# Linear attention, mixture of experts and gated FFN on one core: squares on ScalarE for the weights' scales, unread products in TensorE's pauses, another planned order

## The chip, the cores and the metric

The kernel runs on one core of one Trainium2 chip. The metric is device microseconds (us) of one execution. TensorE (PE) multiplies; VectorE (DVE), ScalarE (ACT) and GpSimd (POOL) do the element work, SyncE (SP) issues the transfers.

## The reference

```python
q_s = exp(q - max_d q); q_s /= sum_d q_s + 1e-9        # q, k, v: (4, 8, 576, 64)
k_s = exp(k - max_s k); k_s /= sum_s k_s + 1e-9        # over the 576 rows
kv  = einsum('bhsd,bhse->bhde', k_s, v)
x   = einsum('bhsd,bhde->bhse', q_s, kv)               # as (2304, 512)
...
P = exp(x @ w_gate - max); 8 rounds of P /= rows' sums, P /= columns' sums, P *= N / E
out = sum_e P[:, e:e+1] * (relu(x @ w1[e]) @ w2[e])    # 8 experts, 512 -> 1024 -> 512
...
h = out @ w_in; g = h * clip(h + 3, 0, 6) / 6; return g @ w_out    # 512 -> 2048 -> 512
```

## The kernel before, in words

**Arithmetic.** A product of fp32 matrices is three fp16 products of high and low halves, and each 2x2 block product takes seven block products instead of four (the forms QA11 to QS3 of a weight, QB11 to QT3 of its partner). So each operand is scaled by a power of two (`pow2`), split (`split`, `sp`) and added into forms. A scale needs the largest absolute value of the whole operand: VectorE reduces along the rows, `across_max` turns the column round with one PE product and reduces it again.

**Tiling.** The 2304 tokens are 6 groups of 384, taken in three pairs, `PAIRS = [(0, 1), (3, 4), (2, 5)]`. The experts are 16 steps (512 columns of one expert's hidden size each), the FFN 4 more; a step takes the pairs one after the other. The weights of step s come by `w1_steps` and `w2_steps`: a load of 1 MB into `raw`, the scale (`w_scale`, L611), splits and sums into `w1buf[s % 2]` or `w2buf[s % 2]`.

**Head.** `attention(0)` works on batches 0 and 1, `attention(1)` on 2 and 3. For keys: `kmax`, `ktr`, `mT`, `kback` (column maxima by way of PE), `ksub`, `kexp`, then `kv` (PE) and `kvout`, `kvmax`, `kvkeep` (its scale). For queries of a group: `qmax`, `qsub`, `qexp`, `qsum`, then per 128 columns `qn` (the norm), `qtr` (PE transposes into a bank, copied out) and `forms` (products with kv, whose forms are operands of step 0). The second pair's queries and the second two batches run beside step 0 (`beside`, `second_pair`).

**Between experts and FFN.** `x2_steps(p)` takes the scale of pair p's result in `acc` (two reduces of 128x1536 on VectorE), scales, turns it round on PE, splits it and adds the FFN's forms.

**The order** is not that of the code. `Planner` (L42) records every instruction (so nearly all show one line, L376 before, L449 after), and `lay` puts them on each engine's queue by modelled costs (`cost`), hops between engines (`hop`) and latest times (`late`, from the time at which the code reaches a PE instruction, backwards). Steps marked as fill go into gaps. The queues are fixed once this is done: an engine does its queue in order, waiting on semaphores.

```python
# L236, order: latest times, then two layings
late = o["at"] + (0.0 if o["eng"] == "tensor" else 10 * self.SLACK if o["fill"] else self.SLACK)
for b in o["post"]:
    late = min(late, b["late"] - o["dur"] - self.hop(o, b))
# L373, issue
for o in self.order():
    for f, a, k in o["calls"]:
        f(*a, **k)
```

Of the kernel before, what the change touches and what calls it, by code (L numbers as in the profile page):

```python
# [36 lines left out]
TOP1 = 12  # L37
TOP2 = 12
H_DOWN = 2.0 ** -21
# [3 lines left out]
class Planner:  # L43
# [10 lines left out]
    GIVE = 100.0  # L54

# [7 lines left out]
    def __init__(self, nc):  # L63
        self.nc = nc
        self.ops = []
        self.clock = 0.0
        self.sb, self.bank = {}, {}
        self.open = None
        self.filling = False
        for e in self.ENGINES:  # L70
            setattr(self, e, Planner.Lane(self, e))
# [56 lines left out]
    def cost(self, eng, name, out, ins):  # L128
# [4 lines left out]
        if eng == "tensor":  # L133
            four = 4 if ins[0].dtype == F32 else 1
            return 2.0 + n * 0.4167 * four
# [22 lines left out]
    def add(self, eng, name, a, k):  # L158
# [4 lines left out]
        ins = [x for x in rest if isinstance(x, bass.AP)]  # L163
        dur = self.cost(eng, name, out, ins)
# [10 lines left out]
        if op is None:  # L175
            op = dict(
                n=len(self.ops), eng=eng, calls=[call], dur=dur, at=self.clock, pre={}, post=[], key=None,
                lock=False, dma=0, name=name, fill=self.filling, out=out.tensor.name,
            )
            self.ops.append(op)  # L180
        if eng == "tensor":
            op["key"] = key
            self.open = op
            self.clock += dur
# [10 lines left out]
        for x, w in [(i, False) for i in ins] + [(out, True)]:  # L195
# [3 lines left out]
    def touch(self, op, x, w):  # L199
        t = x.tensor.name  # L200
        if x.space == bass.MemoryType.PSUM:
            if op is not self.open:
# [24 lines left out]
    def hop(self, a, b):  # L227
# [4 lines left out]
        if a["eng"] == "sync":  # L232
            return 2500.0 + a["dma"] / 150.0
        return self.HOP + (self.MARGIN if b["eng"] == "tensor" else 0.0)

    def order(self):  # L236
# [6 lines left out]
        for o in reversed(ops):  # L243
            late = o["at"] + (0.0 if o["eng"] == "tensor" else 10 * self.SLACK if o["fill"] else self.SLACK)
            for b in o["post"]:
                late = min(late, b["late"] - o["dur"] - self.hop(o, b))
            o["late"] = late
        first = self.lay([o for o in ops if not o["fill"]], None)
# [4 lines left out]
    def lay(self, ops, first):  # L253
# [8 lines left out]
        lag = shift = 0.0  # L262
# [66 lines left out]
        while len(result) < len(ops):  # L329
# [4 lines left out]
            s, o = best[e]  # L334
            if first and o["fill"]:
# [9 lines left out]
            if e == "sync":  # L345
                free[e] = s + 60.0
                end = s
# [25 lines left out]
    def issue(self):  # L373
        for o in self.order():
# [5 lines left out]
def tile_attention_moe_ffn(  # L380
# [170 lines left out]

    def across_max(c, name, st, exact=False):
# [17 lines left out]
    def pow2(m, dst, top):  # L570

        mc = col("mc")
        nc.vector.tensor_scalar(out=mc, in0=m, scalar1=2.0 ** -60, scalar2=2.0 ** 60, op0=ALU.max, op1=ALU.min)
        eb = col("eb", 1, I32)
        nc.vector.tensor_scalar(
            out=eb, in0=mc.bitcast(I32), scalar1=0x7F800000, scalar2=None, op0=ALU.bitwise_and
        )
# [33 lines left out]
    def w_scale(name, st, out_, top, flat=raw):  # L611
        def am(i):
            def f():
                if i == 0:
                    st["am"] = col(f"am_{name}", 2)
                n = NKC * FS // 2
# [6 lines left out]
        def red():  # L623
            st["m"] = col(f"wm_{name}")
            nc.vector.reduce_max(st["m"], st["am"], axis=AX)

        def fin():
            st["s"] = ring("ws", [P, 2], F32, 8)
            pow2(st["mm"], st["s"], top)

        a, gap, b = across_max(lambda: st["m"], name, st)
        return [am(0), am(1), lambda: (red(), a()), gap, b, fin]
# [5 lines left out]
    def w1_steps(s, first=False):  # L638
# [16 lines left out]
        if first:  # L655
            scale = w_scale(f"a{s}_", st, s, TOP1)
# [9 lines left out]
        steps = [load] + fill(s) + w_scale(f"a{s}_", st, s, TOP1)  # L666
# [10 lines left out]
    def w2_steps(s, flat=raw):  # L677
# [10 lines left out]
        steps = [load] + fill(s) + w_scale(f"b{s}_", st, s, TOP2, flat)  # L688
# [99 lines left out]
    def attention(pr):  # L788
# [47 lines left out]
        def vcopy(c, room):  # L836
            hs = slice(2 * c, 2 * c + 2)
            nc.gpsimd.tensor_copy(
# [117 lines left out]
        def qsub(g, eng=nc.vector):  # L956
# [14 lines left out]
        def qn(c, g):  # L971
# [3 lines left out]
            nc.gpsimd.tensor_tensor(  # L975
# [493 lines left out]
    def down_tile(s, p, grp, t, hs):  # L1469
# [21 lines left out]
        leave(s, j)  # L1491
        tick()


# [317 lines left out]
    def x2_steps(p):  # L1812
# [3 lines left out]
        def am(i):  # L1816
            def f():
                if i == 0:
                    st["am"] = col("x2m", 2)
                nc.vector.tensor_reduce(  # L1820
                    out=st["am"][:, i : i + 1],
# [273 lines left out]
```

## Time and profile before

| | us |
|---|---|
| median of 3 runs (1833.99 to 1836.21) | 1836.21 |
| the profiled execution's own time | 1834.17 |
| its span | 1832.4 |
| PE busy, DVE busy | 1778.7, 1446.7 |
| ACT busy, POOL busy | 1041.5, 616.1 |

The span is what the profiler's rows cover; 1.8 us lie around it in the execution's own time. PE is busy for 97% of it, yet busy says that a product was under way, not at which clock: the granted clock (PEclk, 1.00 is 2.4 GHz, 0.50 is 1.2 GHz) is read beside it. The head before the first expert product, the first step and the passage from experts to FFN differ from the rest, so the stretches have to be read apart.

### The profile page before, as it was taken

To read this page: it belongs to the slowest core of one execution; us is meant where nothing else is said; L and a number is where in the kernel's file an instruction comes from. 1 tells how busy PE (TensorE), PEld (TensorE's weight loads), DVE (VectorE), ACT (ScalarE), POOL (GpSimd) and SP (SyncE) were. 2 spreads that over 40 slices of the span, in tenths; PEclk is the share of its full clock that TensorE was granted. 3 is DMA by queue.
4 is the path that set the end of the run, shared out by engine and by line. 5 is a ranking of instruction groups with operands and counts; after the bars stand their busy time and mean duration, and the time that the engine had idled before them with its cause. 6 is when DMAs were issued, how large, how long until landed. Compare 5 with 4: busy or idle time off the path is not lost.

```text
span 1832.4 us, 32369 instructions
## 1 busy us (share of the span) xinstructions
PE 1778.7 (97%) x12858; PEld 1193.4 (65%) x12858; DVE 1446.7 (79%) x2558; ACT 1041.5 (57%) x2231; POOL 616.1 (34%) x581
## 2 busy tenths in 40 slices
PE   4889999999999999999999999999999989999999
PEld 3445555677777777777777777777775545577775
DVE  6975598987888879787888888786986796888674
ACT  2665555555555656555555555655655665665553
POOL 3322425523333242424343332324242434232121
PEclk8899999999999999999999999999999999999999
DMA  8410213131231312131422323131413102302022
GB/s 257 141 66 1 84 59 97 42 110 64 95 102 58 101 58 84 58 120 40 127 69 88 92 68 101 41 101 58 124 36 112 61 24 84 107 1 84 1 89 75
DMA packets 68664, 145.89 MB, mean 80 GB/s; under 512 B 14624, under 2 KB 18720, under 8 KB 68000
## 3 DMA queue, kind: packets, MB, share of 16 engines
q1 hardware_dynamic: 68512, 143.82, 24.5%
q8 instruction: 100, 1.64, 0.4%
q14 instruction: 52, 0.43, 0.1%
HBM read 119.69 MB, written 24.12 MB: 78 GB/s over the span
## 4 chain that ended last, share of the span: by engine, by line
PE 91%; DVE 7%; ACT 1%; issue 1%; DMA 1%; SPq 0%; POOL 0%; DVEq 0%; ACTq 0%; POOLq 0%
PE b L376 91%; DVE xbuf L376 2%; DVE scr L376 1%; DVE ring_qm L376 1%; DVE acc L376 1%; DVE ring_c L376 1%; DVE w2buf L376 1%; DVE ring_r L376 0%; ACT scr L376 0%; DMA acc<-in_v_dram 0%; DVE w1buf L376 0%; SPq L376 0%; DMA acc<-in_q_dram 0%; DVE prob L376 0%; DVE ring_h L376 0%
## 5 line engine op out<-in xcount | busy, mean ns | idle before, releaser
L376 PE MATMUL b<-xbuf,w1buf 128*128 128x384 f16 x5040 | 911.5, 326 | 7.0 <-DVE ring_r L376 6.9
L376 POOL TENSOR_TENSOR ring_h<-ring_r,ring_h 128x384 f16<-128x384 f32 x360 | 352.6, 981 | 997.5 <-ACT ring_h L376 929.7
L376 PE MATMUL b<-w2buf,ring_h 128*128 128x256 f16 (+1 forms) x3756 | 682.5, 316 | 0.9 <-ACT b L376 0.9
L376 PEld LDWEIGHTS <-w1buf 128*128 128x128 f16 x5040 | 491.6, 98 | 286.8 <-issue 10.2
L376 PEld LDWEIGHTS <-ring_h 128*128 128x128 f16 x4320 | 422.3, 98 | 197.1 <-issue 4.6
L376 ACT COPY b<-b 128x256 f32<-128x256 f32 (+1 forms) x658 | 240.2, 375 | 337.4 <-PE b L376 186.0
L376 DVE SCALAR_TENSOR_TENSOR acc<-b,ring_cf,acc 128x512 f32<-128x512 f32 x369 | 274.9, 749 | 131.6 <-PE b L376 118.8
L376 ACT ACTIVATE ring_r<-b 128x384 f32<-128x384 f32 x432 | 211.8, 491 | 194.4 <-PE b L376 191.3
L376 PEld LDWEIGHTS <-xbuf 128*128 128x128 f16 x2436 | 226.2, 98 | 80.9 <-issue 2.0
L376 DVE SCALAR_TENSOR_TENSOR ring_r<-b,ring_r 128x384 f32<-128x384 f32 x282 | 156.0, 553 | 94.4 <-PE b L376 52.6
L376 ACT ACTIVATE ring_h<-ring_r 128x384 f16<-128x384 f32 x330 | 171.2, 522 | 37.7 <-DVE ring_r L376 33.1
L376 DVE TENSOR_TENSOR xbuf<-ring_h 128x768 f16<-128x768 f16 x188 | 122.5, 652 | 1.2 <-POOL ring_h L376 0.8
L376 PE MATMUL b<-xbuf 64*64 64x65 f32 (+1 forms) x1140 | 101.4, 263 | 3.1 <-POOL xbuf L376 1.8
L376 POOL TENSOR_TENSOR scr<-scr 128x512 f32<-128x512 f32 x64 | 85.1, 1329 | 37.7 <-ACT scr L376 33.3
L376 DVE TENSOR_REDUCE ring_c<-raw 128x1 f32<-128x1024 f32 x78 | 92.1, 1208 | 0.0
L376 ACT ACTIVATE ring_r<-ring_r 128x384 f32<-128x384 f32 x114 | 59.7, 523 | 51.7 <-DVE ring_r L376 51.5
L376 PE MATMUL b<-kvs,xbuf 128*128 128x256 f16 x564 | 84.6, 273 | 0.4 <-ACT b L376 0.4
L376 PE MATMUL b<-scr,xbuf 128*128 128x256 f16 x564 | 84.6, 273 | 0.0
L376 PE MATMUL b<-w2buf,xbuf 128*128 128x256 f16 x564 | 84.6, 273 | 0.0
L376 DVE SCALAR_TENSOR_TENSOR w1buf<-raw,ring_ws,w1buf 128x512 f16<-128x512 f32 x100 | 82.8, 860 | 1.0 <-ACT w1buf L376 0.9
L376 DVE SCALAR_TENSOR_TENSOR acc<-b,ring_co,acc 128x512 f32<-128x512 f32 x78 | 57.9, 748 | 30.8 <-PE b L376 28.5
L376 ACT CAST ring_h<-ring_r 128x384 f16<-128x384 f32 x150 | 74.9, 509 | 11.7 <-DVE ring_r L376 10.3
(148 smaller groups left out, 1575.1 us busy)
## 6 DMA issues: line engine op xcount, KB each, us to landing
xbuf<-xkeep SPq DMA_DIRECT2D x119, 384.0 KB, 3.6
raw<-in_moe_w_dram SPq DMA_DIRECT2D x31, 1024.0 KB, 5.5
xkeep<-xbuf SPq DMA_DIRECT2D x4, 2688.0 KB, 8.1
scr<-in_moe_w_in_dram SPq DMA_DIRECT2D x16, 512.0 KB, 3.7
scr<-in_moe_w_out_dram SPq DMA_DIRECT2D x16, 512.0 KB, 3.4
out_dram<-acc SPq DMA_DIRECT2D x18, 256.0 KB, 2.0
win<-scr SPq DMA_DIRECT2D x16, 256.0 KB, 2.6
wout<-scr SPq DMA_DIRECT2D x16, 256.0 KB, 3.3
```

The costliest lines, as they stand in the source:

```text
L376: f(*a, **k)
```

## The change

1. **Weights' scales.** `w_scale` no longer takes absolute maxima on VectorE (two reduces of 128x1024 per set of weights). ScalarE squares the four 128x512 pieces and sums each row's squares on the way (`accum_out`); the squares themselves go to a buffer of forms that is not yet in use. The four columns are added, turned round as before, and `pow2` halves the exponent. 40 sets of weights: 160 ScalarE instructions for 80 VectorE reduces.
2. **Unread products.** `issue(warm)` looks, in the first 130 us of the plan, for pauses of PE over 0.4 us and puts in products of 256 columns (`ones`, `plus`) into a bank that the next reader does not read: 156 pairs of a weight load and a product (71 ahead of the first `kv`, 42 between the last query transposes and the first `forms`, the others in smaller lots).
3. **Planner.** Transfers are modelled as one queue of 350 B/ns; fp32 passes of PE cost more in the model; of two instructions of DVE and POOL that lock each other out the more urgent goes first; a table moves attention's steps to earlier or later (`EARLIER`, `LATER`).
4. **Placement.** Two of the first four copies of v go to ACT, `qsub` of the first pair from DVE to POOL, `qn` (all but 6 of 24) from POOL to DVE.
5. **FFN's input.** The six reduces of 128x1536 become 18 of 128x512, one after the last addition to each 128 tokens (`largest`); latest times of the first PE steps after it are loosened (`X2_LATE`).

```diff
+EARLIER = {"0kexp": -19500.0, ...
+LATER = {"a1scale": 20000.0}
+X2_LATE = (3000.0, 20000.0, 20000.0)
...
             if e == "sync":
                 free[e] = s + 60.0
+                pipe = max(pipe, s + 2000.0) + o["dma"] / 350.0
+                o["land"] = pipe + 2000.0 - s
...
+                if warm and o["start"] < self.WARM and pause > 400:
...
+                    if b:
+                        best = min(b, key=lambda t: seen[t][1] if t in seen else 0.0)
+                        warm(best, int((pause - 150) * self.FILLED[o["start"] > self.COLD] / 109))
...
-    def w_scale(name, st, out_, top, flat=raw):
-        def am(i):
...
-                nc.vector.tensor_reduce(
-                    out=st["am"][:, i : i + 1], in_=flat[:, i * n : (i + 1) * n], axis=AX, op=ALU.max,
-                    apply_absolute_value=True,
...
+    def w_scale(name, st, rest, flat=raw):
+        junk = view(rest, 0, [P, FS], F16)
+
+        def squares(c):
             def f():
+                if c == 0:
+                    st["sq"] = col(f"sq_{name}", NKC)
+                nc.scalar.activation(
+                    junk, flat[:, c * FS : (c + 1) * FS], AF.Square, accum_out=st["sq"][:, c : c + 1]
                 )
             return f
...
-            nc.vector.reduce_max(st["m"], st["am"], axis=AX)
+            nc.vector.tensor_reduce(out=st["m"], in_=st["sq"], axis=AX, op=ALU.add)
...
-            nc.gpsimd.tensor_copy(
+            (nc.scalar.copy if c in (0, 3) else nc.gpsimd.tensor_copy)(
...
-        def qsub(g, eng=nc.vector):
+        def qsub(g):
+            eng = nc.gpsimd if g in PAIRS[0] else nc.vector
...
-            nc.gpsimd.tensor_tensor(
+            (nc.gpsimd if pr == 0 and c % 2 else nc.vector).tensor_tensor(
                 out=t["qn"].rearrange("p (r h d) -> p h r d", h=2, d=D), in0=qof(g)[:, 2 * c : 2 * c + 2],
...
+        if s == NE - 1:
+            largest(p, j)
...
+        nc.vector.tensor_reduce(
+            out=m[:, len(n) - 1 : len(n)], in_=acc[:, j, :], axis=AX, op=ALU.max, apply_absolute_value=True
+        )
...
-                run(x2_steps(pp))
+                run(loosely(x2_steps(pp), X2_LATE[pp]))
...
+            real.tensor.matmul(banks[t][:, : 2 * P], plus, some, start=True, stop=True, skip_group_check=True)
```

**ScalarE, the head.** `xbuf` holds the keys, of 128x1152 per exponential; `acc` of 128x8x192 are a group's queries, `acc` of 128x18x64 two heads' pieces of v, and `ring_h<-b` the copies of the turned queries. Before:

```order
L376 ACTIVATE xbuf<-xbuf 128x1152 x3
L376 ACTIVATE acc<-acc 128x8x192 x2
L376 ACTIVATE xbuf<-xbuf 128x1152
L376 COPY ring_h<-b_67 128x384 x2
L376 COPY ring_h<-b_68 128x384
```

And now:

```order
L449 ACTIVATE xbuf<-xbuf 128x1152
L449 ACTIVATE w1buf_79,ring_c_107<-raw 128x512 x4
L449 ACTIVATE acc<-acc 128x8x192
L449 COPY xbuf<-acc 128x18x64
L449 ACTIVATE xbuf<-xbuf 128x1152
L449 ACTIVATE acc<-acc 128x8x192
L449 COPY xbuf<-acc 128x18x64
L449 COPY ring_h<-b_68 128x384
L449 COPY ring_h<-b_67 128x384
L449 ACTIVATE xbuf<-xbuf 128x1152
```

The four squares of the first weights and two copies of v now stand between the first and the second of the keys' exponentials, and four copies of queries ahead of the last one.

**VectorE, kv of the second two batches**, beside step 0 (`kvs` is kv's normed result, `w2buf_82` the second weights of step 1, `ring_qm` the queries' maxima and sums). Before:

```order
L376 SCALAR_TENSOR_TENSOR ring_h<-ring_r,ring_h 128x384
L376 TENSOR_SCALAR ring_ws<-ring_c1i 128x1
L376 TENSOR_TENSOR ring_wsc<-ring_ws 128x1
L376 SCALAR_TENSOR_TENSOR w2buf_82<-raw,ring_ws,w2buf_82 128x512 x4
L376 TENSOR_SCALAR ring_c_108<-b_68 128x4
L376 TENSOR_SCALAR ring_c_108<-b_67 128x4
L376 RECIPROCAL ring_c_108<-ring_c_108 128x8
L376 TENSOR_TENSOR kvs_89<-b_68,ring_c_108 128x4x64
```

And now:

```order
L449 TENSOR_TENSOR acc<-acc,ring_qm 128x8x192 x2
L449 SCALAR_TENSOR_TENSOR ring_h<-ring_r,ring_h 128x384
L449 TENSOR_REDUCE ring_qm<-acc 128x8x3 x2
L449 TENSOR_SCALAR ring_c_109<-b_68 128x4
L449 TENSOR_SCALAR ring_c_109<-b_67 128x4
L449 RECIPROCAL ring_c_109<-ring_c_109 128x8
L449 TENSOR_TENSOR kvs_89<-b_68,ring_c_109 128x4x64
```

The four splits of `w2buf_82` and the scale that they need came ahead of the norm of kv and now come some twenty rows behind it, one at a time.

**VectorE, the last pair's passage to the FFN** (`acc<-b` are the last additions of the experts, `sx` is the scale). Before:

```order
L376 SCALAR_TENSOR_TENSOR acc<-b_66,ring_cf,acc 128x512
L376 TENSOR_REDUCE ring_c_103<-acc 128x1
L376 TENSOR_REDUCE ring_c_107<-ring_c_103 128x1
L376 TENSOR_REDUCE ring_c_103<-raw 128x1
L376 TENSOR_REDUCE ring_c_107<-b_67 128x1
```

And now:

```order
L449 SCALAR_TENSOR_TENSOR acc<-b_65,ring_cf,acc 128x512
L449 TENSOR_REDUCE ring_x2m<-acc 128x1
L449 SCALAR_TENSOR_TENSOR acc<-b_66,ring_cf,acc 128x512
L449 TENSOR_REDUCE ring_x2m<-acc 128x1
L449 TENSOR_REDUCE ring_c_108<-ring_x2m 128x1
L449 TENSOR_TENSOR xbuf<-scr,xbuf 128x384 x2
L449 TENSOR_REDUCE ring_c_108<-b_67 128x1
```

The long reduce behind the last addition became a short one, and the reduce of weights in `raw` is gone from between.

## Rows read from the trace of the kernel before

**Rows 1.** Stretches: start and length, busy time (instructions) of PE, PEld, DVE, ACT, POOL, PE's clock.

```profile
0.00:32.13 32.13, 8.38 (x210) 6.23 (x210) 22.89 (x30) 8.44 (x9) 10.50 (x15) 0.98 0.85 281
32.13:45.63 13.50, 13.50 (x119) 8.51 (x120) 5.14 (x8) 3.93 (x7) 6.75 (x8) 0.50 0.74 205
45.63:62.61 16.98, 8.93 (x79) 5.04 (x80) 16.48 (x34) 10.01 (x20) 5.12 (x3) 0.70 0.86 243
62.61:103.43 40.82, 39.57 (x450) 23.47 (x449) 38.53 (x59) 30.21 (x52) 11.46 (x11) 0.97 0.19 58
103.43:116.49 13.06, 7.39 (x76) 4.20 (x76) 12.43 (x38) 6.54 (x13) 4.24 (x5) 0.74 0.01 2
...
136.93:1455.11 1318.18, 1315.06 (x9391) 900.90 (x9391) 1057.45 (x1861) 749.20 (x1656) 471.57 (x439) 1.00 0.25 78
1455.11:1500.94 45.83, 44.30 (x258) 25.60 (x256) 42.25 (x82) 32.45 (x65) 16.22 (x15) 1.00 0.10 39
1500.94:1512.55 11.61, 5.45 (x21) 2.48 (x21) 10.55 (x23) 8.36 (x18) 4.11 (x4) 0.71 0.00 1
```

**Rows 2.** PE's waits over the span, by what it waited for: us, times, longest.

```profile
PE b L376 <- DVE scr L376: 13.4, 2, 9.5
...
PE b L376 <- POOL ring_r L376: 6.1, 1, 6.1
PE b L376 <- DVE kvs L376: 5.7, 1, 5.7
```

**Rows 3.** The head's timeline, of POOL and DVE: start, duration, instruction, idle time before it.

```profile
11.90 1.38 POOL L376 COPY xbuf<-acc 128x1152 f32<-128x1152 f32 x1 [10.54 <-DMA acc<-in_v_dram]
...
17.56 1.15 POOL L376 COPY xbuf<-acc 128x1152 f32<-128x1152 f32 x1 [4.27 <-DMA acc<-in_v_dram]
...
23.25 1.28 POOL L376 TENSOR_TENSOR wtmp<-raw 128x512 f32<-128x512 f32 x1 [1.51 <-DMA raw<-in_moe_w_dram]
23.72 5.17 DVE L376 TENSOR_TENSOR acc<-acc,ring_qm 128x1536 f32<-128x1536 f32 x2
24.60 2.67 POOL L376 TENSOR_TENSOR wtmp<-wtmp,raw 128x512 f32<-128x512 f32 x1
31.25 3.20 POOL L376 TENSOR_TENSOR ring_r<-acc,ring_qm 128x384 f32<-128x384 f32 x4 [3.98 <-DVE ring_qm L376]
```

**Rows 4.** Groups of ACT up to 137 us, by shape: count, busy us, mean ns of one.

```profile
L376 ACT ACTIVATE xbuf<-xbuf 128x1152 f32<-128x1152 f32 x8 | 9.2, 1160 | 21.0 <-DVE xbuf L376 20.9
...
L376 ACT ACTIVATE acc<-acc 128x1536 f32<-128x1536 f32 x5 | 7.4, 1485 | 5.8 <-DVE acc L376 5.8
L376 ACT ACTIVATE w1buf<-raw,ring_ws 128x512 f16<-128x512 f32 x10 | 6.7, 712 | 1.1 <-DVE ring_ws L376 1.1
...
L376 ACT COPY ring_h<-b 128x384 f32<-128x384 f32 x8 | 3.8, 475 | 9.8 <-PE b L376 9.8
```

**Rows 5.** Groups of DVE over the whole span.

```profile
L376 DVE TENSOR_REDUCE ring_c<-raw 128x1 f32<-128x1024 f32 x78 | 92.1, 1208 | 0.0
```

**Rows 6.** Groups of ACT over the whole span: splits of weights.

```profile
L376 ACT ACTIVATE w1buf<-raw,ring_ws 128x512 f16<-128x512 f32 x100 | 68.3, 716 | 3.8 <-DVE ring_ws L376 3.2 <-POOL raw L376 0.4
```

**Rows 7.** PE's timeline: the first forms, the last sum ahead of step 0, the two later gaps.

```profile
50.70 3.52 PE L376 MATMUL b<-ring_h,xbuf 64*64 64x192 f32 x40 [1.66 <-DVE xbuf L376]
...
62.61 1.44 PE L376 MATMUL b<-xbuf,minus 128*128 128x384 f16 x4 [2.23 <-DVE xbuf L376]
...
113.06 0.87 PE L376 MATMUL b<-ident,xbuf 128*128 128x128 f32 x3 [5.67 <-DVE kvs L376]
...
1509.54 2.08 PE L376 MATMUL b<-xbuf,w1buf 128*128 128x384 f16 x6 [6.16 <-DVE ring_r L376]
```

**Rows 8.** The passage to the FFN, all engines: PE at full clock, and a reduce of weights.

```profile
1489.75 1.63 PE L376 MATMUL b<-xbuf,w1buf 128*128 128x384 f16 x9
...
1494.11 1.21 DVE L376 TENSOR_REDUCE ring_c<-raw 128x1 f32<-128x1024 f32 x1
...
1494.84 1.14 PE L376 MATMUL b<-xbuf,w1buf 128*128 128x384 f16 x6
```

More of the change, by code (lines that the diff above doesn't have):

```diff
@@ L163, in add @@
         ins = [x for x in rest if isinstance(x, bass.AP)]
+        sums = k.get("accum_out")
+        ins = [x for x in ins if x is not sums]
         dur = self.cost(eng, name, out, ins)
@@ L177, in add @@
                 n=len(self.ops), eng=eng, calls=[call], dur=dur, at=self.clock, pre={}, post=[], key=None,
-                lock=False, dma=0, name=name, fill=self.filling, out=out.tensor.name,
+                lock=False, dma=0, name=name, fill=self.filling, loose=self.loose, mark=self.mark,
+                out=out.tensor.name,
             )
             self.ops.append(op)
+            op["banks"] = set()
+            op["anew"] = eng == "tensor" and (name == "transpose" or bool(k.get("start")))
         if eng == "tensor":
@@ L194, in add @@
         )
-        for x, w in [(i, False) for i in ins] + [(out, True)]:
+        for x, w in [(i, False) for i in ins] + [(x, True) for x in (out, sums) if x is not None]:
             self.touch(op, x, w)
@@ L247, in order @@
             o["late"] = late
+        for o in ops:
+            o["late"] -= EARLIER.get(o["mark"], 0.0)
         first = self.lay([o for o in ops if not o["fill"]], None)
@@ L334, in lay @@
             s, o = best[e]
+            if o["lock"]:
+                r = best[other[e]]
+                if r is not None and r[1]["lock"] and r[0] <= s + 100 and r[1]["late"] < o["late"]:
+                    e = other[e]
+                    s, o = r
             if first and o["fill"]:
@@ L549, in filling, with marked, g, loosely @@
         return f and g
+    def marked(f, key):
+        def g(*a, **k):
+            was, nc.mark = nc.mark, key
+            r = f(*a, **k)
+            nc.mark = was
+            return r
+        return g
+    def loosely(steps, by):
+        def one(f):
+            def g():
+                nc.loose = by
+                f()
+                nc.loose = 0.0
+            return f and g
+        return [one(f) for f in steps]
     def across_max(c, name, st, exact=False):
@@ L1861, in tile_attention_moe_ffn, with tag, one, g @@
         t0, t1 = attention(0), attention(1)
+        for t in (t0, t1):
+            for key, f in list(t.items()):
+                if callable(f) and key != "items":
+                    t[key] = marked(f, ("0" if t is t0 else "1") + key)
+        def tag(steps, key):
+            def one(f):
+                def g():
+                    was, nc.loose = nc.loose, LATER.get(key, 0.0)
+                    marked(f, key)()
+                    nc.loose = was
+                return f and g
+            return [one(f) for f in steps]
         K = call(t0)
```

146 lines of the change are left out of this document (103 added, 43 removed).

## The prediction

> **What bounds the kernel now.** I read the stretches first [rows 1]. The reader should set PE's busy time against each length and look at the clock. From 136.93 to 1455.11, 72% of the span, PE is busy for 1315.06 of 1318.18 us at a clock of 1.00: 3.1 us idle, so nothing that spares VectorE or GpSimd can shorten this stretch, whatever it saves there. The rest is different. Before 62.61 PE is idle for 23.75 + 0 + 8.05 = 31.8 us, and the 13.50 us from 32.13, in which it never pauses, run at 0.50, 1.2 GHz. From 62.61 to 116.49 it is idle for 1.25 + 5.67 us, from 1455.11 to 1512.55 for 1.53 + 6.16. Whatever the change brings must come from these places.
>
> Then the waits [rows 2] and PE's timeline [rows 7] say what it waits for there. In the head: VectorE's column maxima (13.4 in two waits), GpSimd's first normed queries (6.1), VectorE's sums of forms. At 113.06: kv's norm on VectorE (5.67). At 1509.54: VectorE (6.16). VectorE is busy for 38.53 of 40.82 us ahead of the second of these gaps and 42.25 of 45.83 ahead of the third: it has fallen behind there, and the wait is its backlog.
>
> **The change part by part.**
>
> *A. Head.* Transfers first. Between the first and the third piece of v (copies at 11.90 and 17.56 [rows 3]) two pieces of v of 288 KB and eight of q of 192 KB land: 2112 KB in 5.66 us, 2.74 us a MB. The first weights landed behind all of v, at 23.25 (`wtmp`'s start, released by that transfer). Now the eight pieces of v, 2.25 MB, come behind them: 2.25 x 2.74 = 6.2 earlier, about 17.1. The queries come before that, so they no longer decide.
>
> ScalarE's queue from then on is the longest chain. Up to the last exponential of the keys it holds four squares, two exponentials of queries, two copies of v, three exponentials of keys and four copies of queries. Squares aren't in the trace. Below they are bounded by a copy of 384 columns (475 ns), above by the exponential of 1152 (1160), and a split of the same 512 columns took 712 mean, ten in 6.7 us [rows 4]; I take 0.67. The copies of v I put at an exponential of the same 1152 columns. So 4 x 0.67 + 2 x 1.48 + 2 x 1.16 + 3 x 1.16 + 4 x 0.47 = 13.4, and the chain ends at about 30.6. GpSimd's `qsub` of 2 x 1536 columns lies beside it: four pieces of 384 took 3.20 [rows 3], which is 3.2 for one group, so the two groups would be done at about 22.6, ahead of ScalarE's need. The last products of keys and values and the last turned queries then need about 3.0 at full clock: `kv` ends at 33.6, not 45.63.
>
> The unread products are to keep the clock up through this. Nine products of 384 columns took 1.63 and six 1.14 [rows 8], so one takes 0.163 and one of 256 columns 0.109, 0.218 at half clock. The 71 ahead of the first `kv` stand where PE idles for 23.75 us anyway and cost nothing. The 42 behind the last turned queries take 4.6 us, in a stretch where PE before waited 5.07 (45.63 to 50.70 [rows 1, 7]) for kv's norm and scale on VectorE. Half of them stand ahead of the turning of kv's maximum, which is then about 0.6 late; so I take 5.7 for that stretch, and the forms start at 39.3. From there to the last sum it took 11.91 [rows 7]. Two reduces of weights at 1.21 [rows 5] stood in VectorE's way, PE's own part ran at 0.5 for most of it, and what VectorE has to do there now is five splits at 0.67 and seven sums at 0.50, 7.2 in all with small change; the bounds are 7.2 and 9.5 (only the reduces gone). I take 7.2: this point, at 62.61, is reached at 46.5, **16.1 earlier**. The half clock behind it ends too: 3% of 40.82 us [rows 1], 1.2. Against it stand the smaller lots of unread products and what they delay, some 14 where PE would have run on: 1.5. **A is 16** (bounds 8, if ScalarE's and VectorE's chains only shift, and 19).
>
> *B. Kv of the second two batches.* Available: 1.25 + 5.67 idle, and 7.39 us at 0.74, 1.9: 8.8. Ahead of that norm VectorE's queue loses four reduces of weights (4.8) and four splits with their scale (3.5), and the sums that ran beside them now come earlier (3.1): of some 50 us from 59.76 on about 38 are left. Counted from the point at 46.5 the norm is then done at about 86 to 88; PE, with 44.8 us of products and pauses from that point to the gap (62.61 to 107.4), would ask for it at about 90. So the gap could vanish. But ScalarE, busy for 30.21 of the 40.82 us, gets eight squares (5.4) and is then at 87%, VectorE gets part of the norms of queries (18 over the whole run), and the order is planned to use what it gains. I give back 4 of the 8.8: **B is 5** (0 to 9).
>
> *C. Passage to the FFN.* Available: 1.53 + 6.16 idle and 5.45 us at 0.71, 1.6: 9.2. The reduces of weights that stood in the passage (1.21 each, one behind the last addition [rows 8], one 4 us before it) leave VectorE; six reduces become eighteen of a third each, of which only the last stands behind the last addition (about 0.6 for 1.75). This spares VectorE some 5 of its 42.25 us, and the plan is allowed to put the last pair's steps later. **C is 7** (0 to 9.2).
>
> *D. The rest.* 92.1 us of reduces leave VectorE [rows 5], and some 144 squares at 0.67, about 97 us, enter ScalarE, which has 749.20 busy of 1318.18. Cover: PE's 3.1 us of idle time, and a queue on ScalarE that is 57% full, then 63%. If a square stood ahead of a copy that PE waits for, the price would be up to one square each time. I take 0, with 1.5 either way.
>
> Sum: 16 + 5 + 7 = 28. The profiled execution took 1834.17 us, its span was 1832.4; the median of the runs is 2.0 above it. 1832.4 - 28 = 1804.4; with the 1.8 around the span 1806.2; a median about a us above that: **1807**.
>
> **A rule against the change.** The granted clock was 0.50 from 32.13 to 45.63 with PE busy the whole time [rows 1]: what ran were fp32 products of 65 columns and fp32 transposes. Unread products in the pauses before don't change this mix. The Trainium skill, "TensorE: Matmul & The Clock Gate", Part 4, says that PE-mode transposes don't count as busy for the clock in the way other products do; the row agrees so far as PE's being busy didn't raise the clock, and cannot say which instruction was to blame.
>
> **Rivals.**
>
> 1. *The clock falls in spite of the unread products.* For it: the stretch just named. Against: here `kv` is fed in as exponentials arrive, with most of its products done before, and full-width fp16 products now stand right ahead of and behind it. Price: 42 products at 0.218 instead of 0.109, 4.6, and about 1.2 for the rest of `kv`: 28 - 5.8 = 22, **1813**. Chance 0.17.
>
> 2. *Backlogs stay the bound.* ScalarE, with squares and v, is late instead of VectorE, the head wins only its transfers and the two reduces (8), kv's norm none and the passage as forecast: 15, **1820**. For it: ScalarE's 13.4 us chain has no slack, and VectorE is at 94% in step 0. Against: what leaves VectorE is more than what enters it. Chance 0.15.
>
> 3. *GpSimd's `qsub` is locked out by VectorE.* `wtmp` took 2.67 us beside a VectorE subtraction of two operands in SBUF, 1.28 without [rows 3]. If both `qsub` are doubled, the second ends at 29 and the chain at about 35: 4.4 lost, **1811**. Against: from 16 to 23 us VectorE now has reduces and sums from PSUM; the copies on GpSimd beside those took 1.15. The Trainium skill, "SBUF — State Buffer", "SBUF: two separate sides", calls the pair of ports an exclusive lock, against a VectorE instruction with two inputs in SBUF; the 2.67 agrees with that. Chance 0.04.
>
> 4. *Slower: squares ahead of what PE waits for.* ScalarE's queue is fixed. Each of the 36 later sets of weights puts four squares into it, 2.7 us, and `b<-b` copies and reliefs of banks behind a square come up to 0.67 late. To eat 28 us, 144 squares would have to cost PE 0.2 us each, and the run is slower by more than that only if the mean is, say, 0.35: 50 - 28 = 22 slower, **1858**. Against it: 100 splits of the same size in the same queue, 716 ns each [rows 6], and PE idle for 3.1 us in all. Chance 0.06, with other mishaps.
>
> 5. *Nothing is left:* what the head wins is waited for again in step 0, since its end is set by transfers and ScalarE, and the passage stays. **1836**. Chance 0.03.
>
> **How the numbers follow.** The forecast has 0.55, its own range 1799 to 1812 from A's, B's and C's bounds, not all at one end. Rivals 1, 3 and 2 at 1813, 1811, 1820 belong into a range that leaves out 0.2: **1794 to 1822** (below, all three terms near their upper bounds, 37, would give 1798, and D's 1.5 and a better passage a few less). About 0.2%, 3.7 us, is what a measurement of this kernel can tell from no change. Faster by more than that: 0.55 + 0.17 + 0.15 + 0.04 = 0.91, I say 0.90; within: 0.04; slower: 0.06.
>
> **What would show it.** Right: squares near 0.67; ScalarE's last exponential of keys at about 30 us; `kv` over at about 34; forms from 39; the sum of 62.61 at 46 to 47; a clock near 1.00 all the way from 30 us; kv's norm at 86 to 88 and no pause of 5 us behind it; no pause of 6 us between experts and FFN; PE's idle time in the long stretch still about 3 us. A clock of 0.50 between 25 and 40 us is rival 1; the sum of 62.61 at 52 or later, with ScalarE or VectorE in PE's waits, rival 2; `qsub` of over 3 us a group rival 3; PE waiting for ScalarE's copies dozens of times in the long stretch rival 4. The forecast is wrong if the head's gain is under 10 or if a new pause takes the place of one of the three gaps.

## The result and the profile after

| | before | changed |
|---|---|---|
| median (lowest to highest) | 1835.72 (1833.99 to 1836.21) | 1811.93 (1811.23 to 1812.85) |
| the profiled execution's own time, its span | 1834.17, 1832.4 | 1812.85, 1811.1 |
| PE, DVE, ACT busy | 1778.7, 1446.7, 1041.5 | 1785.4, 1365.9, 1144.8 |

The ratio is 0.9872 (95% interval 0.9855 to 0.9889): 23.8 us between the medians, 21.3 between the two spans (the profiled execution of the kernel before is 1.6 under its median, that of the changed kernel 0.9 above its own), where 28 were forecast. The time lies in the range. The page of the changed kernel, busy shares and the granted clock:

```profile
PE 1785.4 (99%) x13014; PEld 1201.5 (66%) x13014; DVE 1365.9 (75%) x2506; ACT 1144.8 (63%) x2553; POOL 598.5 (33%) x563
...
PEclk9999999999999999999999999999999999999999
```

PE's busy time rose although the kernel is shorter: the 156 unread products count in it. The stretches answer to [rows 1] (columns as there):

```profile
0.00:22.68 22.68, 12.60 (x92) 8.88 (x92) 15.43 (x26) 8.51 (x16) 7.07 (x10) 1.00 0.93 325
22.68:34.91 12.23, 11.13 (x325) 8.96 (x326) 9.07 (x14) 8.64 (x12) 8.36 (x9) 1.00 0.84 195
34.91:48.49 13.58, 12.65 (x140) 9.48 (x137) 11.81 (x32) 11.50 (x26) 2.68 (x2) 1.00 1.01 269
48.49:55.34 6.85, 2.87 (x20) 1.67 (x17) 2.45 (x8) 2.16 (x7) 1.32 (x2) 1.00 0.98 289
55.34:75.00 19.66, 19.66 (x124) 11.73 (x124) 15.79 (x31) 16.43 (x36) 9.36 (x6) 0.91 0.26 73
75.00:99.98 24.98, 24.69 (x393) 14.57 (x392) 24.84 (x28) 18.85 (x34) 7.12 (x6) 1.00 0.46 170
...
120.00:1437.06 1317.06, 1314.51 (x9385) 899.26 (x9384) 998.33 (x1814) 831.27 (x1910) 463.82 (x434) 1.00 0.24 77
...
1473.26:1482.34 9.08, 6.91 (x44) 4.33 (x44) 7.51 (x24) 7.12 (x17) 1.91 (x2) 1.00 0.01 2
```

Keys, values and queries no longer run at half clock (second line; 13.50 us at 0.50 before), and the passage to the FFN has 2.2 us of pauses (last line) where one of 6.16 stood. The fourth line is new: in 6.85 us PE works for 2.87. Where the lead comes from shows when the same expert product is timed in both traces, counted in PE's order (products that read `w1buf` or `w2buf`):

| product | before | changed | lead |
|---|---|---|---|
| 1st | 63.85 | 48.49 | 15.4 |
| 13th | 67.81 | 55.34 | 12.5 |
| 101st | 83.08 | 75.48 | 7.6 |
| 201st | 117.42 | 99.98 | 17.4 |
| 7201st | 1411.23 | 1396.34 | 14.9 |
| 7701st | 1523.65 | 1501.21 | 22.4 |
| last | 1828.24 | 1806.64 | 21.6 |

So the head gave 15.4, 7.8 of it are lost by the 101st product, the second batches gave 9.8 back, the long stretch lost 2.6, the passage gave 7.5, the FFN lost 0.8. The count leaves out what else PE has done by then: ahead of the 201st product the kernel before had made nine turns of queries (`ident,xbuf`), 1.4 us, that the changed kernel makes later. PE's waits, against [rows 2]:

```profile
PE b L449 <- DVE scr L449: 7.2, 2, 6.4
PE b L449 <- ACT ring_r L449: 5.2, 3, 4.0
PE b L449 <- DVE ring_c L449: 5.2, 7, 1.4
```

The waits for GpSimd's queries (6.1) and kv's norm (5.7) are gone; one for ScalarE is new. ScalarE's timeline, in the head and around 54 us:

```profile
17.22 0.63 ACT L449 ACTIVATE w1buf<-raw 128x512 f16<-128x512 f32 x1 [5.17 <-DMA raw<-in_moe_w_dram]
17.75 0.19 ACT L449 ACTIVATION_READ_ACCUMULATOR w1buf<-raw 128x1 f32 x1
17.97 0.63 ACT L449 ACTIVATE w1buf<-raw 128x512 f16<-128x512 f32 x1
...
28.98 1.18 ACT L449 ACTIVATE xbuf<-xbuf 128x1152 f32<-128x1152 f32 x1
...
53.81 0.63 ACT L449 ACTIVATE w1buf<-raw 128x512 f16<-128x512 f32 x1 [4.69 <-DMA raw<-in_moe_w_dram]
54.34 0.19 ACT L449 ACTIVATION_READ_ACCUMULATOR w1buf<-raw 128x1 f32 x1
54.44 0.46 ACT L449 CAST xbuf<-b 128x384 f16<-128x384 f32 x1
54.80 0.49 ACT L449 ACTIVATE ring_r<-b 128x384 f32<-128x384 f32 x1
```

and PE's, at the first expert products:

```profile
48.49 1.14 PE L449 MATMUL b<-xbuf,w1buf 128*128 128x384 f16 x6
...
55.34 1.26 PE L449 MATMUL b<-xbuf,w1buf 128*128 128x384 f16 x6 [3.98 <-ACT ring_r L449]
```

A square is two instructions, the square and the reading of its sum, and four of them come 0.75 us apart. The last exponential of keys ends at 30.16 (forecast 30.6). At 53.81 a square of step 1's first weights has waited 4.69 us for its transfer; the copy and the relief behind it, which PE needs, waited with it.

### The profile page after: what moved, and what is told of

It reads as the page before. It is cut to its first block, busy times and chain, and to the rows that moved or that the text cites. A ratio compares the mean times of both kernels' runs of the same rounds, so it can differ in the third digit from the quotient of the medians.

```text
span 1811.1 us, 32922 instructions
## 1 busy us (share of the span) xinstructions
PE 1785.4 (99%) x13014; PEld 1201.5 (66%) x13014; DVE 1365.9 (75%) x2506; ACT 1144.8 (63%) x2553; POOL 598.5 (33%) x563
## 4 chain that ended last, share of the span: by engine, by line
PE 94%; DMA 2%; ACT 2%; DVE 1%; issue 0%; SPq 0%; POOL 0%; ACTq 0%; POOLq 0%; DVEq 0%
PE b L449 94%; ACT w2buf L449 1%; DMA raw<-in_moe_w_dram 1%; DMA acc<-in_moe_w_dram 0%; DMA acc<-in_v_dram 0%; DMA xbuf<-in_k_dram 0%; DMA acc<-in_q_dram 0%; DVE xbuf L449 0%; DVE ring_r L449 0%; DVE ring_qm L449 0%; ACT ring_r L449 0%; ACT w1buf L449 0%; DVE prob L449 0%; ACT scr L449 0%; ACT ring_h L449 0%
## 5 line engine op out<-in xcount | busy, mean ns | idle before, releaser
L449 PE MATMUL b<-xbuf 64*64 64x65 f32 (+1 forms) x1140 | 96.4, 247 | 0.8 <-ACT xbuf L449 0.5
L449 DVE TENSOR_SCALAR scr<-scr 128x512 int32<-128x512 int32 x160 | 73.7, 477 | 1.2 <-issue 0.3
```

## Experiments

Each compares with the kernel before, run beside it; its medians were 1835.1 to 1835.5, so the experiments' medians can be set against 1811.9. A plan made anew moves many instructions, which is why each is also read at the products of the table above. Even one order varies from execution to execution. The run with the old passage to the FFN (below) has the changed kernel's order, instruction by instruction on every engine, up to that passage, and in its trace the 1st expert product comes 1.0 us earlier and the 201st 3.8. Its pause at the 13th product:

```profile
53.86 1.14 PE L449 MATMUL b<-xbuf,w1buf 128*128 128x384 f16 x6 [3.51 <-ACT ring_r L449]
```

Behind this pause of 3.51 us the clock stayed at 1.00; behind the 3.98 us of the changed kernel's trace it was at 0.50 for 3.4 us. So a lead of under 4 us in the head, read from one trace each, isn't shown to come from an edit. Unless said otherwise the edit is to the changed kernel.

### Without unread products

```diff
-        nc.issue(warm)
+        nc.issue()
```

> The changed kernel without its 156 unread products; every other instruction stands as it did. Theory (they keep the clock up): the granted clock falls to 0.50 somewhere between 20 and 35 us and stays there; the stretch from 22.7 to 34.9 us, some 9.9 us of PE's own work at full clock, takes up to 9.9 longer, of which the 5 us of unread products behind it and the pause of 3.98 us at 51 us give some back: 4 to 9 us slower than the changed kernel, 1816 to 1821. Rival (they cost more than they give): the clock stays at 1.00 or falls for a few us only, and the 85 unread products behind the first product of keys and values, 85 x 0.109 = 9.3 us, were partly in the way: 1 to 4 us faster than the changed kernel, 1808 to 1811.

1811.6 (1809.0 to 1813.4), ratio 0.9870 (0.9856 to 0.9885): the same. The 1st product comes 0.5 us earlier, the 201st 1.5, and it stays so; that is within what one order varies by. The first products of keys and values, in this run and in the changed kernel, and two stretches of this run:

```profile
22.59 3.38 PE L449 MATMUL b<-xbuf 64*64 64x65 f32 x118 [2.38 <-ACT xbuf L449]
```

```profile
22.68 1.28 PE L449 MATMUL b<-xbuf 64*64 64x65 f32 x72 [0.46 <-ACT xbuf L449]
```

```profile
25.70:34.30 8.60, 7.49 (x206) 5.74 (x201) 5.58 (x8) 5.59 (x10) 5.75 (x5) 1.00 0.90 246
34.30:48.00 13.70, 8.33 (x83) 4.58 (x82) 12.17 (x34) 11.31 (x27) 3.19 (x3) 0.88 1.13 290
```

The unread products do act on the clock. Without them the first products of keys and values take 0.029 us each where they took 0.018 (of this run the trace has no clock ahead of 25.7), there is some half clock from 34 to 48 (0.88), and from 53.0, within the pause at 51 us, there is 6.8 us of it instead of 3.4. But the last turned queries come at 34.4 us here and at 34.5 there, and unread products take PE's time at other places; the sum is nil. The fp32 products and transposes from 25.7 on run at full clock with nothing put in. In the kernel before such work ran at 0.50 from 32.13, straight behind 6.1 us in which PE did nothing. So it isn't the unread products that undid this stretch. Two things differ from the kernel before: that pause is gone, and the mix is not the same (173 products of keys and values and 21 transposes in these 8.6 us, 98 and 21 in those 13.5). Which of the two counts, no run separates. The rival's direction is what was seen, its size is within the noise.

### Unread products in the kernel before

```diff
-    def issue(self):
-        for o in self.order():
+    def issue(self, warm=None):
...
+        nc.issue(warm)
```

> The kernel before with unread products in its planned pauses, everything else in its order. Theory (where PE idles for 6.1 us ahead of 32.13, unread products keep the clock up): the 13.5 us at 0.50 from 32.13 become 7 to 9, the first expert product comes 3 to 7 us earlier, the time 3 to 7 us under the kernel before. Rival (as in the changed kernel, where leaving them out changed nothing): within 1.5 us of the kernel before, the clock at 0.50 in the same place.

1834.9 (1831.4 to 1836.6), ratio 0.9997 (0.9987 to 1.0006): nothing, as the rival has it. PE still pauses for 5.3 us ahead of the queries, at 31.87, and runs at 0.50 behind it; the pause is not in the plan, so nothing is put there. So the theory, unread products in that very pause, wasn't tried by this run.

### The squares that wait, moved behind

```diff
         ops = self.order()
+        ours = [o for o in ops if o["mark"] == "w11" and any("accum_out" in k for f, a, k in o["calls"])]
+        ops = [o for o in ops if o not in ours]
+        at = next(i for i, o in enumerate(ops) if o["eng"] == "vector" and ours[0]["n"] in o["pre"])
+        ops[at:at] = ours
```

> The changed kernel with one thing moved on one engine: the four squares of step 1's first weights, which wait on ScalarE for a transfer that lands at 53.8 us, stand behind the three copies and the two reliefs of banks that followed the first of them. Theory (a square that waits for its transfer holds up copies that PE needs): the pause of 3.98 us at 51.4 us goes, and with it the 3.4 us at half clock behind it (1.7): 3 to 6 us faster than the changed kernel, 1806 to 1809. Rival (that pause only hides a later one, as the weights of step 1 come late in any case): the pause moves to where step 1's weights or the second batches' keys are first needed, within 1 us of the changed kernel.

1813.2 (1812.4 to 1815.4), ratio 0.9882 (0.9867 to 0.9897): the rival's time, but not its cause. PE's timeline, then GpSimd's and ScalarE's:

```profile
50.41 1.14 PE L453 MATMUL b<-xbuf,w1buf 128*128 128x384 f16 x6
...
54.20 2.11 PE L453 MATMUL b<-xbuf,w1buf 128*128 128x384 f16 x12
60.72 0.23 PE L453 MATMUL b<-identb,ring_c 128*128 128x128 bf16 x1 [4.40 <-DVE ring_c L453]
```

```profile
52.61 2.28 POOL L453 TENSOR_TENSOR wtmp<-raw 128x512 f32<-128x512 f32 x1 [13.02 <-DMA raw<-in_moe_w_dram]
...
56.19 1.26 POOL L453 TENSOR_TENSOR raw<-raw 128x512 f32<-128x512 f32 x1
```

```profile
57.49 0.63 ACT L453 ACTIVATE w1buf<-raw 128x512 f16<-128x512 f32 x1 [4.00 <-POOL raw L453]
```

The pause of 3.98 is gone, the lead at the 31st product is 6.6 us larger, and at 60.72 PE waits 4.40 us for the product that turns the scale of these weights round, which stands in its own queue. The weights aren't what is late: they land at 52.6, when GpSimd starts on them. The edit did more than was meant. It put the squares behind GpSimd's subtraction as well, which writes into the same buffer (`raw<-raw`), so that the first square starts only when that ends, 4.00 us after ScalarE was free (and the squares are taken of partly subtracted weights). So this run decides neither for the theory nor for the rival.

### A plan with slower transfers, with and without unread products

```diff
-                pipe = max(pipe, s + 2000.0) + o["dma"] / 350.0
+                pipe = max(pipe, s + 2000.0) + o["dma"] / 250.0
```

> The changed kernel planned with transfers at 250 bytes per ns instead of 350, nothing else. The plan then puts the squares of step 1's first weights behind six more copies and reliefs on ScalarE, and the product that turns their scale round behind 54 instead of 36 expert products. Theory (the pause at 51 us comes from a plan that takes those weights to land some 4 us earlier than they do): the pause falls under 1 us and does not come back before 100 us: 3 to 6 us faster than the changed kernel, 1806 to 1809. Rival (what is late is the weights themselves, and PE runs out of other work): a pause of the same sum at another place before 100 us, within 1.5 us.

> The kernel planned with transfers at 250 bytes per ns, without its 228 unread products; all else in the same order. Theory (there 43 unread products between 49.8 and 75 us, 4.7 us, stand where PE had work, which is why the pause at 51 us went without a gain): 3 to 6 us faster than the changed kernel, 1806 to 1809, and the lead of 6 us at the 60th expert product holds to the 200th. Rival (the weights of step 1, or the second batches, are late in any case): pauses take the place of the unread products, 1810 to 1813.

1811.9 (1810.9 to 1813.4), ratio 0.9873 (0.9859 to 0.9888), and 1812.6 (1810.9 to 1813.5), ratio 0.9878 (0.9864 to 0.9893): the rivals' times, both. No pause over 0.5 us is left from 22 to 90 us in the first, and at the 61st product it is 6.1 us ahead of the changed kernel: the weights of step 1 are not late for a plan that takes their transfer to be slower. But at the 201st it is 0.2 ahead. In between stand 34 unread products, 3.7 us, where the changed kernel has none, and pauses of 1.46 and 0.58 us behind 90 us, where that has one of 0.29. I suspected the unread products after 49.8 (39 in the trace, not the 43 that I had counted); without them the lead still shrinks, from 5.2 to 0.7, and pauses stand in their place. Of the kernel without them, PE's timeline and a stretch:

```profile
64.47 1.14 PE L449 MATMUL b<-xbuf,w1buf 128*128 128x384 f16 x6 [0.97 <-ACT ring_r L449]
75.19 1.14 PE L449 MATMUL b<-xbuf,w1buf 128*128 128x384 f16 x6 [1.86 <-ACT ring_r L449]
```

```profile
60.00:77.00 17.00, 14.07 (x94) 8.41 (x93) 15.43 (x25) 16.56 (x34) 7.92 (x7) 1.00 0.19 62
```

ScalarE is busy for 16.56 of 17.00 us there, and PE waits for it. So the pause at 51 us can be planned away, and in step 0 ScalarE then has no room to make use of it. Between the 61st and the 201st product the pauses come to 3.9 us, for 0.3 in the changed kernel; one of them, 0.84 at 93.48, ends with nothing that the profile shows. Another 0.4 are four turns of the second batches' maxima, which the changed kernel makes ahead of the 61st product. That is 4.0 of the 4.5 us that vanish.

### Largest values on VectorE again, everywhere

```diff
-        return [*map(squares, range(NKC)), lambda: (red(), a()), gap, b, fin]
+        return [am(0), None, am(1), None, lambda: (red_old(), a()), gap, b, fin_old]
```

> The changed kernel with all 40 weights' scales taken from largest absolute values on VectorE again (two reduces of 1.2 us each), and planned anew; unread products, tables, placement and the passage to the FFN as changed. Theory (the squares are worth what VectorE's backlog cost in step 0, less what they cost ScalarE): the 9 us won between 93 and 117 us shrink to between 0 and 5, the pause of 3.98 us at 51 us goes, the 2 us of pauses in the long stretch go: between 1 us faster and 6 us slower than the changed kernel, 1811 to 1818. Rival A (squares carry the gain): the gap ahead of the second batches' kv opens again in full, 8 us or more slower, 1820 or more. Rival B (squares are a net loss): 3 us or more faster, 1809 or less.

1816.7 (1815.1 to 1818.1), ratio 0.9899 (0.9884 to 0.9914): 4.8 us slower than the changed kernel, inside the theory's range. Against the changed kernel it is 2.8 us late at the 1st product, 3.4 late at the 201st, 1.1 *early* at the 7501st, and 2.8 late again behind the passage. In between it is 5.1 early at the 61st product, as the pause of 3.98 is gone without squares, and loses that and more up to the 201st: the second batches' 9.8 shrink to 4.6, as the theory has it. So by this trace the squares gain about 3 in the head and 4 in the passage, and cost 4.5 in between; the 3 are no more than one order varies by, while the runs behind the 4.8 between the medians don't overlap.

### Largest values on VectorE for steps 2 to 14

```diff
+        if name[0] in "ab" and 2 <= int(name[1:-1]) <= 14:
+            return [am(0), None, am(1), None, lambda: (red_old(), a()), gap, b, fin_old]
```

> The changed kernel with the scales of steps 2 to 14 taken from largest values on VectorE again; squares stay for steps 0, 1 and 15 to 19. Theory (in the long stretch the squares cost PE time: four in a row, 0.74 us apart, stand ahead of copies and of the product that turns a scale round, and pauses of 0.99, 0.56, 0.56 us stand behind them): from the point at 200 to 1455 us 3 to 5 us are won, 1807 to 1809, and the pauses on the scale's column (ring_c) in that stretch are gone. Rival (those pauses are chance of the plan, the same total is waited for elsewhere): within 1.5 us of the changed kernel.

1810.5 (1808.9 to 1811.2), ratio 0.9864 (0.9849 to 0.9879). What it undoes is seen in the changed kernel at one of three such places, on ScalarE and then on PE:

```profile
1126.61 0.63 ACT L449 ACTIVATE w2buf<-raw 128x512 f16<-128x512 f32 x1
1127.15 0.19 ACT L449 ACTIVATION_READ_ACCUMULATOR w2buf<-raw 128x1 f32 x1
1127.24 1.01 ACT L449 COPY b<-b 128x384 f32<-128x384 f32 x3
```

```profile
1127.58 0.23 PE L449 MATMUL b<-identb,ring_c 128*128 128x128 bf16 x1 [0.56 <-DVE ring_c L449]
```

The last of four squares ends at 1127.3, and PE has stood for 0.56 us before the product that turns the sums round; three copies of banks came behind the squares. With steps 2 to 14 on VectorE these pauses are gone, and from the 201st to the 6501st product 4.1 us are won, as the theory said; 2.4 are lost again up to the 7201st, behind step 14, where squares come back. What is left, 1.4 us between the medians, is inside both intervals: the theory is right on the stretch, and the time is the rival's.

### The passage to the FFN as before

```diff
-X2_LATE = (3000.0, 20000.0, 20000.0)
+X2_LATE = (0.0, 0.0, 0.0)
...
-        if s == NE - 1:
-            largest(p, j)
...
+        steps = [am(0), am(1), lambda: (red(), a()), gap, b, lambda: pow2(st["mm"], sx[:, p, :], TOP1)]
```

> The changed kernel with the passage to the FFN as before (six reduces of 128x1536, no loosened times), all else as changed, planned anew. Theory (the late reduces and the tight times made that gap): of the 7.5 us won there 4 to 7 are lost again, 1816 to 1819, with a pause of PE of 3 us or more ahead of the FFN's last pair. Rival (the gap went because the weights' reduces left VectorE): within 2 us of the changed kernel, no pause over 1.5 us there.

1815.5 (1813.9 to 1818.0), ratio 0.9897 (0.9881 to 0.9914): 3.6 slower, just under the theory's 1816. Between the 7201st and the 7701st product 4.4 us are lost. PE pauses more often there, 4.5 us in all for 2.2, though no pause is 3 us long, and the clock falls to 0.50 for 3.4 us, which it doesn't in the changed kernel:

```profile
1476.52 0.55 PE L449 MATMUL b<-ident,acc 128*128 128x128 f32 x3 [0.88 <-ACT scr L449]
1478.43 3.66 PE L449 MATMUL b<-xbuf,w1buf 128*128 128x384 f16 x12 [1.37 <-DVE ring_r L449]
```

```profile
1478.80:1482.20 3.40, 3.40 (x13) 1.81 (x12) 2.82 (x7) 2.70 (x7) 0.69 (x1) 0.50 0.00 0
```

So of the 7.5 us in the passage, about 4 belong to the late reduces with the loosened times.

### Empty tables

```diff
-EARLIER = {"0kexp": -19500.0, ...
+EARLIER = {}
-LATER = {"a1scale": 20000.0}
+LATER = {}
```

> The changed kernel with the two tables that move attention's steps emptied, planned anew. Theory (the head's gain of 15.4 us at the first expert product comes from the order that the tables set, transfers first of all): 5 to 12 us of it are lost, the first expert product comes at 53 to 60 us, 1817 to 1824. Rival (it comes from squares, placement and the model of the transfers): the first expert product within 2 us of 48.5, the time within 3 us of the changed kernel.

1825.9 (1825.4 to 1827.5), ratio 0.9952 (0.9935 to 0.9969). The theory, and more than it had: the 1st product comes at 57.97, 9.5 us later, and 14.0 us are lost between the medians. PE's timeline begins with

```profile
21.00 0.45 PE L429 MATMUL b<-ident,scr 128*128 128x128 f32 x1 [21.00 <-DVE scr L429]
```

where the changed kernel's first product starts at 6.43: without the table the plan loads the queries first, and the keys' maxima come 14.6 us later.

### The placement of before

```diff
-            (nc.scalar.copy if c in (0, 3) else nc.gpsimd.tensor_copy)(
+            nc.gpsimd.tensor_copy(
...
-            eng = nc.gpsimd if g in PAIRS[0] else nc.vector
+            eng = nc.vector
...
-            (nc.gpsimd if pr == 0 and c % 2 else nc.vector).tensor_tensor(
+            nc.gpsimd.tensor_tensor(
```

> The changed kernel with the placement of before: the copies of v on GpSimd, the queries' subtraction on VectorE, the queries' norms on GpSimd; planned anew, the tables kept. Theory (VectorE's backlog in the head was worth time: two subtractions of 1.75 to 2.6 us go back to it): the first expert product comes 3 to 6 us later, the whole 3 to 7 us, 1815 to 1819. Rival (with the reduces of weights gone VectorE has room, and ScalarE gets two copies fewer): within 2 us of the changed kernel.

1821.2 (1819.6 to 1821.4), ratio 0.9925 (0.9910 to 0.9939): 9.2 slower, more than the theory had. PE's timeline:

```profile
45.26 3.81 PE L449 MATMUL b<-ring_h,xbuf 64*64 64x192 f32 x48 [2.98 <-DVE ring_c L449]
49.01 5.66 PE L2190 MATMUL b<-ones,plus 128*128 128x256 f16 x47
```

The first forms start at 45.26, 5.4 us later, the plan leaves a pause of over 5 us behind them (filled here with 47 unread products), and the 1st expert product comes 10.4 later. The direction is shown; how much of the 9.2 is the placement itself and how much this plan's pause, I can't tell.

### Squares alone, in the kernel before

```diff
-        return [am(0), am(1), lambda: (red(), a()), gap, b, fin]
+        return [*map(squares, range(NKC)), lambda: (red(), a()), gap, b, fin]
```

> The kernel before with squares on ScalarE for all weights' scales, planned anew by its own planner; nothing else of the change. Theory (the reduces of weights were VectorE's backlog in step 0 and in the passage to the FFN): the pause of 5.67 us at 113 us shrinks by 3 or more, that of 6.16 us at 1509 us by 1 to 5, pauses of 1 to 3 us come up in the long stretch: 3 to 9 us faster than the kernel before, 1826 to 1832. Rival (without the tables the squares only move the backlog to ScalarE): within 2 us of the kernel before, or slower.

1841.4 (1840.4 to 1844.1), ratio 1.0040 (1.0025 to 1.0054): *slower* by 5.8 us, the rival. PE's waits:

```profile
PE b L379 <- DVE ring_c L379: 13.3, 7, 6.0
...
PE b L379 <- POOL wtmp L379: 7.2, 1, 7.2
...
PE b L379 <- ACT scr L379: 6.0, 7, 3.5
```

The pause at 112 us is as long as ever (6.03), now on a scale's column, that in the passage is shorter (3.47 for 6.16), and the long stretch loses 7.6 us between the 201st and the 7501st product. Squares take a load from VectorE; what this is worth depends on an order that uses it.

### Both repairs together

```diff
-                pipe = max(pipe, s + 2000.0) + o["dma"] / 350.0
+                pipe = max(pipe, s + 2000.0) + o["dma"] / 250.0
...
+        if name[0] in "ab" and 2 <= int(name[1:-1]) <= 14:
+            return [am(0), None, am(1), None, lambda: (red_old(), a()), gap, b, fin_old]
...
-        nc.issue(warm)
+        nc.issue()
```

> The kernel planned with transfers at 250 bytes per ns, without unread products, with largest values on VectorE for steps 2 to 14. Theory (the two losses are apart, one in the head, one in the long stretch): their gains add, 4 us and 2 to 4 us, 1803 to 1807. Rival (no gain in the head): 1808 to 1811, as with the squares of steps 2 to 14 alone.

1808.7 (1807.8 to 1809.0), ratio 0.9858 (0.9843 to 0.9872). It is the lowest of all medians, 3.2 us under the changed kernel's, and its runs don't overlap with that kernel's; the two intervals do, so it is likely, not certain, that it beats it. The lead comes from the long stretch alone (4.8 us at the 6501st product, none at the 201st), as its rival had it for the head.

## Why the prediction was right, and where it was off

The time, 1811.9 for 1807, would suit rivals 1 and 3 (1813, 1811) as well; only the traces tell them from the forecast. That the sum came so near is in part luck: A was 8.4 us too large and B 4.8 too small, and these set each other off. By the forecast's own sign it was half wrong: the head's gain is over 10 at the first expert product and under it at the 101st, and a new pause, of 3.98 us, came up behind the head.

**The head, up to the first expert product: right in place and size.** Step by step: the first weights land at 17.2 (forecast 17.1); ScalarE's chain ends at 30.2 (30.6), with squares at 0.75 apart instead of 0.67, and that is set off by smaller steps elsewhere; GpSimd's two subtractions end at 22.0 (22.6), 2.78 each; the last product of keys, values and turned queries ends at 34.9 (33.6); forms start at 39.8 (39.3); the sum of 62.61 comes at 47.4 (46.5). That the last turned queries are 1.3 late and the forms only 0.5 is luck: the stretch between them took 4.9 us for 5.7. The tables carry the larger part of the gain: without them 9.5 of 15.4 us are gone. Without the new placement 10.4 are gone; the two together are more than the whole, so each needs the other, or the plan made anew adds to it.

**Term A as a whole was too large, 16 for 7.6 at the 101st product.** I let the head's lead run on into step 0. It met step 1's weights, which land at 53.8: ScalarE's square waits for them with PE's copies behind it, 3.98 us of pause, and the clock is at half for 3.4 us behind it (0.91 over the stretch from 55.34), about 1.0 more than the half clock cost the kernel before here. This is the mechanism of rival 4, a square ahead of what PE waits for, at a place and of a kind that I hadn't priced: not a square's own 0.7 us, but its wait for a transfer. Ten unread products between the 1st and the 101st product took 1.25. The rest of the 7.8 is products that the kernel before made earlier or later. The half clock is chance in part: in the run with the old passage, of the same order, the lead over the kernel before is 10.8 at the 101st product. That this order makes the pause is shown by planning the transfer later, and by the run without squares: both have none there. That its going brings nothing by itself is shown by the first of these; ScalarE, full from 60 to 77 us, is what PE waits for then. Rival 5, that step 0 takes the head's gain back, had half of it.

**Term B was too small, 5 for 9.8.** The gap is gone, with 0.3 us left. My step for it failed all the same: kv's norm is done at 99.1, not 86 to 88, as VectorE is busy for 24.84 of the 24.98 us from 75 on. PE doesn't ask at 90 either. It gets expert products of steps 0 and 1 and the second batches' keys and values first, and comes to the product for kv's scale at 100.63 without a wait:

```profile
98.31 0.76 DVE L449 TENSOR_TENSOR kvs<-b,ring_c 128x256 f32<-128x256 f32 x2
```

```profile
100.63 0.22 PE L449 MATMUL b<-identb,ring_c 128*128 128x128 bf16 x1
```

The 4 us that I gave back for ScalarE's squares weren't lost here, and 1.4 of the 9.8 are the nine turns of queries that come later now. A and B together gave 17.4 for the 21 forecast, 21.2 in the trace of the same order with the old passage.

**Term C was right: 7.5 for 7.** About 4 of it come from the late reduces and loosened times; from the squares, by the run without any, 3.9. The two parts were measured in different plans.

**Term D was off: minus 3.4 for 0 with 1.5 either way.** Of the 2.6 in the long stretch about 1 is order, the nine turns again. Pauses of 0.99, 0.56 and 0.56 us, all on a scale's column behind four squares in a row, are gone where steps 2 to 14 use VectorE, and 4.1 us are won there. Yet PE's pauses between the 201st and the 7201st product are no more than before, 2.6 us for 3.4: the squares' pauses took the place of others, and what removed those no run shows. The cover that I named, PE's 3.1 us of idle time and ScalarE at 57%, was an average; at three places the squares were what came last. The price, 4.1 us over the 104 squares of those steps, is 0.04 us each, a fifth of where rival 4 would have eaten the gain.

**Rival 1 fell.** The clock was at 1.00 from 25.7 to 39.3 even without unread products, with fp32 products and transposes in turn, so such work doesn't keep it low by itself; the mix was not quite that of [rows 1], and the clock was up when this part of it began. The Trainium skill, "TensorE: Matmul & The Clock Gate", Part 4, from which the rival took its support, speaks of transposes alone; with products between them this run can't say whether it holds. Rival 2 was half right: ScalarE is the bound from 60 to 77 us, in step 0, once the pause at 51 us is planned away. Rival 3 fell in the head: the two subtractions took 2.78 us each, under the 3.20 that I had put and the 3 that would have been its sign. What it describes is seen at 56.51, below.

## What to carry to other kernels

An instruction that waits for a transfer holds up everything behind it on its engine; when work is moved to another engine, look first at what stands behind it there while its input is on the way. An engine's average share is no cover: the squares were free at most places and cost time at the few where they came last. And a change of load is worth what the order makes of it: the same squares cost 5.8 us in the old order and were worth 4.8 in the new one, while unread products to hold the clock were worth nothing here, where the pause itself was gone. And before a few us in one trace are put down to an edit, look what two executions of one order differ by: here 3.8.

## What was not expected of the hardware

A sum taken along with an activation is a second instruction: 0.19 us for each reading of the accumulator behind 0.63 for the square, so that four squares of 128x512 come 0.75 us apart, while splits of the same size took 0.71 each [rows 4] and ten of them 6.7 us. And GpSimd's subtraction of 1536 elements took 2.78 us as one instruction, against 3.20 for four multiplications of 384 [rows 3]. One of 128x512, 1.27 us at most other places, took 3.32 beside a VectorE instruction with both operands in SBUF, and ended 1.13 us behind the end of that; whether this cost PE anything isn't shown:

```profile
56.33 2.37 DVE L449 TENSOR_TENSOR scr<-xbuf 128x2048 f32<-128x2048 f32 x1
...
56.51 3.32 POOL L449 TENSOR_TENSOR raw<-raw 128x512 f32<-128x512 f32 x1
```
